# Nine zero products ahead of the first transposes, a last weight chunk of 128 rows, transposes two blocks ahead, and new durations in a hand-written order model

## The chip, the core and the metric

The kernel runs on one core of a Trainium2 chip. The metric is the device time of one execution in microseconds (us). Five engines work side by side, each through its own instructions in order: TensorE (PE, with its weight loads shown as PEld), VectorE (DVE), ScalarE (ACT), GpSimd (POOL) and SyncE (SP), which here issues nearly all DMAs. They meet through semaphores.

## What is computed

The reference normalizes x (2048 rows of 512) and adds two branches to it:

```python
xn = layernorm(x)
# A: attention, 32 heads of 16, each row sees itself and the 255 rows before it
q, k, v = split(xn @ wqkv)
o = softmax(mask(q @ k.T * 16**-0.5)) @ v
# B: gated mixer, 688 columns in each half
z = gelu(xn @ w_in);  z1, z2 = z[:, :688], layernorm(z[:, 688:])
g = w_sp @ z2 + b_sp[:, None]
out = x + o @ wo + (z1 * g) @ w_out
```

Inputs and output are bfloat16.

## The kernel before

The 2048 rows are 16 blocks of 128. The work has three stages.

**Front** (lines 326 to 516). For each block n, VectorE takes the statistics of x (`x_stats`, L387 and L388), adds the epsilon (L259), POOL raises to the power -0.5 (L260), and VectorE applies both (`norm_apply`, L392) and writes `xn`. `transpose_x(n)` turns it to `xnT`: for blocks 0 to 7 by four TensorE transposes (L406) and a ScalarE copy (L409), from block 8 on (`X_DMA = 8`) by a DMA transpose (L401). `do_z(n, half)` multiplies `xnT` by one half of `w_in` (L417; 512 and 176 columns by four chunks) into PSUM tiles of the pool `ps_s`, and ScalarE applies gelu (L425). For the half with z2, VectorE takes statistics (L265) and normalizes (L269). A loop runs n from 2 to 18: the z2 half of block n, the norm of block n + 3, a transpose, the statistics of earlier z2 and later x blocks, one unit of the first k, q, v projections from n = 6 on, and the z1 half of block n - 3. `small_setup` gives POOL three memsets and a small DMA.

**Main stage** (lines 518 to 718). The units are issued in an order that the class `Plan` writes while the program is built:
- `quad(kb, G, e)`: four score products over 32 rows (L623) into two `ps_s` tiles of three, and two exponentials on ScalarE (L631). `mask` clears E on POOL (L640) and, for blocks 0 to 13, on VectorE (L645).
- `unit_av`: 48 small products (L658) into the one bank of `ps_y`, then on VectorE a transpose, a reciprocal, a product and a transpose (L667 to L680).
- `unit_k`, `unit_q`, `unit_v`: projections into the same bank of `ps_y`, read out by VectorE (L290, L310, L324).
- `unit_g(n, hf, c)`: one of 16 products (L545) of half hf of block n of the mixer, 344 columns, into the one bank of `ps_g`; behind the sixteenth VectorE writes `u_sb` (L552) and frees the bank; behind the second half a DMA transpose makes `uT`.
- `unit_out(n, part)`: part 0 adds four products with `wo` (L585), part 1 six with `w_out` (L593) into one `ps_y` bank; VectorE adds x (L597) and SP writes the block. FH is 688, so the last of six chunks has 48 rows.

`Plan` keeps a time for TensorE, VectorE, ScalarE and POOL and adds a constant for each unit. At each step it chooses, among the units whose inputs and bank it takes to be ready, the one of the best rank; `g` products are the filler of the lowest rank. `OUT_MM` is its time of one output product, `self.td += ...` behind an "av" the VectorE time after the bank has been read.

**Tail** (lines 719 to 721). The last three blocks' outputs (`TAIL_OUT = 3`) run behind everything else, in `ps_s` tiles; ScalarE's queue issues their writes.

The buffers of `u_sb` are 768 columns wide and columns 688 to 767 are zero (L379), so that `uT` has zeros in rows 48 to 127 of its last chunk.

Of the kernel before, what the change touches and what calls it, by code (L numbers as in the profile page):

```python
# [8 lines left out]
P = 128  # L9
BF = mybir.dt.bfloat16  # L10
F32 = mybir.dt.float32
# [8 lines left out]
FH = 688  # L20
# [7 lines left out]
NFC = UPAD // P  # L28
# [3 lines left out]
EBUFS = 12  # L32
X_DMA = 8
TAIL_OUT = 3


def nblk(kb):
# [3 lines left out]
class Plan:  # L41
# [1 line left out]

    PROJ = 0.91
    AV_PAIR = 0.0165
    OUT_MM = 0.24
    GCH = 0.144
    LAT = 0.36
    BACK = 0.08
# [13 lines left out]
    def run(self, proj, n_out_inline):  # L63
# [17 lines left out]
        while qi < len(quads) or ai < len(avs) or oi < len(outs) or gi < len(gs) or proj:  # L81
# [13 lines left out]
            if qi < len(quads):  # L95
                kb, G, e = quads[qi]
                ok = True
                if e == 0:
                    i = 4 * kb + G - EBUFS
# [15 lines left out]
            if ai < len(avs):  # L115
                qb, h = avs[ai]
                keys = [(kb, G) for kb in range(max(0, qb - 2), qb + 1) for G in (2 * h, 2 * h + 1)]
                if all(k in masked for k in keys) and not any(
# [3 lines left out]
                    n = sum(1 for k in keys) * 8  # L122
# [8 lines left out]
            if oi < len(outs):  # L131
                n, part = outs[oi]
# [5 lines left out]
            if gi < len(gs):  # L138
                n, hf, c = gs[gi]
# [16 lines left out]
            if pick[2] == "quad":  # L156
                kb, G, e = quads[qi]
                w = nblk(kb)
                order.append(("quad", kb, G, e))
                a, b = (2 * qi) % 3, (2 * qi + 1) % 3  # L160
                dur = {3: 0.755, 2: 0.55, 1: 0.34}[w]
                lat = self.LAT - 0.05 * (3 - w)
                for s in (a, b):
                    self.ta = max(self.ta, self.tp + lat) + dur
                    self.sfree[s] = self.ta + self.BACK
                self.tp += 0.14 + 0.054 * w
                if e == 1:
                    pend.append((self.ta + 0.05, (kb, G)))
                qi += 1
            elif pick[2] == "av":  # L170
                qb, h = avs[ai]
                order.append(("av", qb, h))
                self.tp += pick[3]
                self.yfree = self.evac(0.75)
                self.td += 0.85
                if h == 1:
                    o_at[qb] = self.td + 0.1
                av_emitted.add((qb, h))
                ai += 1
            elif pick[2] == "proj":  # L180
                p = pick[4]
                proj.remove(p)
                order.append(("proj", p[2], p[3]))
                self.tp += pick[3]
                self.yfree = self.evac({"k": 1.2, "q": 0.7, "v": 0.7}[p[2]])
                done_proj[(p[2],) + p[3]] = self.yfree
            elif pick[2] == "out":
                n, part = outs[oi]
                order.append(("out", n, part))
                self.tp += pick[3]  # L190
                if part == 1:
                    self.yfree = self.evac(0.7)
                oi += 1
            else:
                n, hf, c = gs[gi]
                order.append(("g", n, hf, c))
                self.tp += self.GCH
                if c == NB - 1:
                    self.gfree = self.evac(0.52)
                    if hf == 1:  # L200
                        u_at[n] = self.gfree + 3.0
                gi += 1
# [6 lines left out]
def kernel(  # L209
# [12 lines left out]
    nc = tc.nc  # L222
# [6 lines left out]
    xnT = pers.tile([P, NDC, S_TOK], BF, name="xnT")  # L229
    wqkv = pers.tile([P, NDC, 3 * D], BF, name="wqkv")  # L230
    wo_sb = pers.tile([P, NDC, D], BF, name="wo_sb")
    w_out_sb = pers.tile([P, NFC, D], BF, name="w_out_sb")
# [16 lines left out]
    ps_s = ctx.enter_context(tc.tile_pool(name="ps_s", bufs=3, space=bass.MemoryType.PSUM))  # L249
    ps_y = ctx.enter_context(tc.tile_pool(name="ps_y", bufs=1, space=bass.MemoryType.PSUM))  # L250
    ps_g = ctx.enter_context(tc.tile_pool(name="ps_g", bufs=1, space=bass.MemoryType.PSUM))
# [60 lines left out]
    def unit_v(n, on_act=False):  # L312
# [10 lines left out]
        else:  # L323
            nc.vector.tensor_copy(out=dst, in_=src)  # L324

    nc.vector.memset(fmask[:], 1.0)
    nc.vector.memset(esel[:], 1.0)
    make_identity(nc, ident[:])
    with tc.tile_pool(name="win_pool", bufs=1) as winp, tc.tile_pool(
        name="xsp", bufs=8  # L330
# [18 lines left out]
        def load_win(half, c0=0, c1=NDC):  # L349
# [15 lines left out]
            out=fmask[:], in_=fmask[:], pattern=[[-1, P]], compare_op=ALU.is_gt,  # L365
# [7 lines left out]
            out=esel[:], in_=esel[:], pattern=[[32, 4]], compare_op=ALU.is_ge,  # L373
            fill=0.0, base=DH - 1, channel_multiplier=-1,
        )
        def small_setup():
            nc.gpsimd.memset(v_ring[:, :, :, 1, :], 1.0)
            for u_sb in u_sbs:
                nc.gpsimd.memset(u_sb[:, FH:UPAD], 0.0)  # L379
            with nc.allow_non_contiguous_dma(reason="tiny bias gather"):  # L380
                nc.gpsimd.dma_start(out=b_bf[:], in_=B_b_sp.rearrange("(n p) -> p n", p=P))

        xn_tiles = {}

# [5 lines left out]
        def norm_apply(n):  # L390
            xn = xnp.tile([P, D], BF, name="xn")
            nc.vector.tensor_scalar(  # L392
                out=xn[:], in0=xs_tiles[n], scalar1=mvx[:, n, 0:1],
                scalar2=rstdx[:, n : n + 1], op0=ALU.subtract, op1=ALU.mult,
            )
            xn_tiles[n] = xn

        def transpose_x(n):
            xn = xn_tiles.pop(n)
            if n >= X_DMA:  # L400
                nc.sync.dma_start_transpose(out=xnT[:, :, n * P : (n + 1) * P], in_=xn[:])  # L401
                return
            pool, tag = (ps_y, "y") if n in (1, 3) else (ps_g, "g")
            tp = pool.tile([P, NDC, P], BF, name="tp", tag=tag)
            for c in range(NDC):
                nc.tensor.transpose(  # L406
                    out=tp[:, c, :], in_=xn[:, c * P : (c + 1) * P], identity=ident[:]
                )
            nc.scalar.copy(out=xnT[:, :, n * P : (n + 1) * P], in_=tp[:])  # L409

        def do_z(n, half):
            zp2 = ps_s.tile([P, 2, 512], F32, name="zs", tag="S")
            zp = zp2[:].rearrange("p a q -> p (a q)")
            f0 = half * FH
            for c in range(NDC):
                for lo, hi in Z_RANGES:
                    nc.tensor.matmul(  # L417
                        zp[:, lo:hi],
                        lhsT=xnT[:, c, n * P : (n + 1) * P],
                        rhs=w_in_sb[:, c, f0 + lo : f0 + hi],  # L420
                        start=(c == 0),
                        stop=(c == NDC - 1),
                    )
            dst = z1_all if half == 0 else z2_all
            nc.scalar.activation(out=dst[:, n, :], in_=zp[:, 0:FH], func=ACT.Gelu_apprx_tanh)  # L425
# [40 lines left out]
        nc.sync.dma_start(  # L466
            out=w_out_sb[:, 0:5, :], in_=B_w_out[0:640, :].rearrange("(c p) n -> p c n", p=P)
        )
        nc.sync.dma_start(out=w_out_sb[0:48, 5, :], in_=B_w_out[640:688, :])
        norm_apply(2)  # L470
        rs_x(3, 4)
        do_z(0, 1)
        norm_apply(3)
        do_z(1, 1)
        small_setup()
        transpose_x(2)
        x_stats(4)
        transpose_x(3)
        rs_x(4, 5)
        nc.vector.tensor_reduce(  # L480
            out=emask[:, 0:1], in_=esel[:], op=ALU.add, axis=mybir.AxisListType.X
# [9 lines left out]
        for n in range(2, NB + 3):  # L491
            if n < NB:
                do_z(n, 1)
            if n + 3 < NB:
                norm_apply(n + 3)
                if n + 3 >= X_DMA:
                    transpose_x(n + 3)
            if 3 <= n < X_DMA - 1:
                transpose_x(n + 1)
            if n == 4:  # L500
                nc.vector.tensor_copy(out=b_all[:], in_=b_bf[:])
            if 1 <= n - 1 < NB:
                z2_side(n - 1)
            if n + 4 < NB:
                x_stats(n + 4)
                rs_x(n + 4, n + 5)
            if n >= 6 and early:
                f, a = early.pop(0)
                f(*a, on_act=True)
            if n >= 3:  # L510
                do_z(n - 3, 0)
# [60 lines left out]
    def unit_out(n, part, tail=False):  # L572
        if part == 0:
            if not tail:
                load_xres(n)
            if tail:
                t = ps_s.tile([P, 2, 512], F32, name="mt", tag="S")
                fo_tiles[n] = t[:, 0, :]
            else:
                t = ps_y.tile([P, 512], F32, name="fo", tag="y")  # L580
                fo_tiles[n] = t[:]
            fo = fo_tiles[n]
            for c in range(NDC):
                oT = oT_tiles[(n, c // 2)]
                nc.tensor.matmul(  # L585
                    fo, lhsT=oT[:, c % 2, :], rhs=wo_sb[:, c, :], start=(c == 0), stop=False
                )
            return
        fo = fo_tiles.pop(n)
        uT = uT_tiles.pop(n)  # L590
        for c in range(NFC):
            kk = P if c < NFC - 1 else FH - (NFC - 1) * P
            nc.tensor.matmul(  # L593
                fo, lhsT=uT[0:kk, c, :], rhs=w_out_sb[0:kk, c, :], start=False, stop=(c == NFC - 1)
            )
        x_ch = x_tiles.pop(n)
        nc.vector.tensor_tensor(out=x_ch, in0=fo, in1=x_ch, op=ALU.add)  # L597
        (nc.scalar if tail else nc.sync).dma_start(out=out2[n * P : (n + 1) * P, :], in_=x_ch)
        if n + 1 < NB - TAIL_OUT:
            load_xres(n + 1)  # L600
# [151 lines left out]
```

## Time and profile before

| what | value |
|---|---|
| time, median of 3 runs | 295.42 us (295.39 to 295.44) |
| profiled execution: time, span | 295.57 us, 293.9 us |
| PE, DVE, ACT, POOL busy in the span | 269.4, 213.9, 218.2, 92.8 us |
| chain of waits, by engine | PE 64%, DVE 25%, issue 4%, POOL 3% |
| front, main stage, tail | to 61.1, 61.1 to 282.9, to 293.9 us |
| output products L593, score products L623, g products L545 | 96, 576, 512 |

The span runs from the first to the last instruction of the profile. The profile shows matmuls with their latency, so they overlap: how fast TensorE goes is seen from one start to the next. In timeline rows the columns are start, length, engine, line, operation, tiles, shape, count, and in brackets the idle time before it and what ended it. A shape of 48*128 is a product over 48 rows into 128 columns of weights; the rest is the moving operand, so that 48x512 means 48 rows by 512 columns. Some matmul records can be missing, so that rows can show a few too few.

### The profile page before, as it was taken

How to read it: one execution, taken by the hardware profiler on the slowest of the kernel's cores; microseconds unless marked ns; L12 is line 12 of the kernel's file. 1: busy time of each engine (PE TensorE's matmuls, PEld its weight loads, DVE VectorE, ACT ScalarE, POOL GpSimd, SP SyncE). 2: the span in 40 equal slices, each digit the busy share in tenths (PEclk: the TensorE clock that was granted, in tenths of full speed). 3: DMA queues.
4: the chain of work that ended last, by engine and by line, in shares of the span. 5: the costliest groups of instructions: out<-in, count | busy, mean ns of one | idle time of the engine just before them, and what ended most of it. 6: DMA issues, size and time to landing. Idle time of an engine off the chain costs nothing.

```text
span 293.9 us, 7526 instructions
## 1 busy us (share of the span) xinstructions
PE 269.4 (92%) x3136; PEld 135.5 (46%) x3168; DVE 213.9 (73%) x412; ACT 218.2 (74%) x314; POOL 92.8 (32%) x102
## 2 busy tenths in 40 slices
PE   1899999999989989999998999999898999999895
PEld 0555544444435444444544453545444554545451
DVE  5877777936877685865788887866869885956681
ACT  2478756588889889988699958783797678798810
POOL 3622222203342234324143323333233312335520
PEclk9999999999999999999999999999999999999999
DMA  7991111800415242332231423144314133545103
GB/s 230 324 284 44 36 38 36 170 12 0 100 19 118 65 72 51 89 85 51 65 74 39 99 44 94 39 97 56 83 36 100 31 70 83 94 38 134 29 4 80
DMA packets 60178, 23.58 MB, mean 80 GB/s; under 512 B 51264, under 2 KB 59632, under 8 KB 60144
## 3 DMA queue, kind: packets, MB, share of 16 engines
q1 hardware_dynamic: 59664, 22.70, 34.0%
q8 instruction: 25, 0.41, 0.6%
q10 hardware_dynamic: 432, 0.39, 0.4%
q0 software_dynamic: 48, 0.00, 0.1%
q14 instruction: 9, 0.07, 0.1%
HBM read 8.41 MB, written 2.10 MB: 36 GB/s over the span
## 4 chain that ended last, share of the span: by engine, by line
PE 64%; DVE 25%; issue 4%; POOL 3%; DMA 2%; ACT 1%; SPq 0%; DVEq 0%
PE gf L545 23%; PE S L623 9%; PE o_t L658 7%; PE fo L593 7%; PE fo L585 4%; PE m L315 4%; DVE st L265 3%; PE m L300 3%; DVE o_norm L673 3%; DVE st L387 3%; DVE o_c L667 3%; PE m L277 3%; DVE E L645 3%; POOL rstdx L260 2%; PE zs L417 2%
## 5 line engine op out<-in xcount | busy, mean ns | idle before, releaser
L631 ACT ACTIVATE E<-S 128x768 bf16<-128x768 f32 (+2 forms) x256 | 178.9, 773 | 38.4 <-issue 22.6
L640 POOL TENSOR_SCALAR_AFFINE_SELECT E<-E 128x1024 bf16<-128x1024 bf16 x64 | 74.7, 1167 | 147.9 <-ACT E L631 122.3
L545 PE MATMUL gf<-z_all,wspT 128*128 128x344 bf16 x512 | 94.6, 311 | 6.1 <-DVE u_sb L552 6.1
L545 PEld LDWEIGHTS <-wspT 128*128 128x128 bf16 x512 | 44.3, 97 | 38.4 <-issue 15.8
L645 DVE TENSOR_TENSOR E<-E,fmask 128x1024 bf16<-128x1024 bf16 x56 | 47.6, 853 | 0.6
L623 PE MATMUL S<-q_ring,k_ring 32*128 32x384 bf16 (+2 forms) x576 | 45.2, 303 | 1.3 <-ACT E L631 1.2
L417 PE MATMUL zs<-w_in_sb,xnT 128*128 128x512 bf16 (+1 forms) x251 | 42.5, 318 | 2.5 <-DMA xnT<-xn 1.3
L425 ACT ACTIVATE z_all<-zs 128x688 bf16<-128x688 f32 x32 | 23.8, 744 | 17.1 <-PE zs L417 17.1
L667 DVE STREAM_TRANSPOSE o_c<-o_t 128x512 f32<-128x512 f32 x32 | 22.9, 715 | 15.2 <-PE o_t L658 14.9
L417 PEld LDWEIGHTS <-xnT 128*128 128x128 bf16 x256 | 22.7, 101 | 20.9 <-DMA xnT<-xn 3.1
L623 PEld LDWEIGHTS <-k_ring 32*128 32x128 bf16 x576 | 14.6, 91 | 38.3 <-issue 36.0
L658 PE MATMUL o_t<-E,v_ring 128*32 128x128 bf16 x1440 | 26.0, 220 | 1.0 <-DVE k_ring L290 0.8
L658 PEld LDWEIGHTS <-v_ring 128*32 128x32 bf16 x1440 | 20.9, 97 | 8.2 <-issue 7.7
L597 DVE TENSOR_TENSOR x_ch<-fo,x_ch 128x512 bf16<-128x512 f32 x13 | 9.0, 692 | 21.2 <-PE fo L593 18.6
L673 DVE TENSOR_TENSOR o_norm<-o_c,rsum 128x256 bf16<-128x256 f32 x32 | 21.4, 668 | 1.1
L593 PE MATMUL fo<-w_out_sb,uT 128*128 128x512 bf16 x78 | 20.4, 382 | 0.0
L552 DVE SCALAR_TENSOR_TENSOR u_sb<-gf,b_all,z_all 128x344 bf16<-128x344 f32 x32 | 17.9, 560 | 1.7 <-PE gf L545 1.5
L290 DVE TENSOR_TENSOR k_ring<-m,emask 128x1024 bf16<-128x1024 f32 x12 | 14.7, 1221 | 5.8 <-PE m L277 5.8
L315 PE MATMUL m<-wqkv,xnT 128*128 128x512 bf16 x53 | 15.9, 381 | 1.1 <-DVE x_ch L597 0.5
L300 PE MATMUL m<-xnT,wqkv 128*128 128x512 bf16 x58 | 16.2, 380 | 0.7 <-DVE v_ring L324 0.3
L277 PE MATMUL m<-xnT,wqkv 128*128 128x512 bf16 x57 | 16.1, 380 | 0.6 <-DVE o_c L667 0.2
L260 POOL TENSOR_TENSOR rstdx<-rs_v,negh 128x1 f32<-128x1 f32 x16 | 8.8, 550 | 23.6 <-DVE rs_v L259 22.2
(51 smaller groups left out, 175.9 us busy)
## 6 DMA issues: line engine op xcount, KB each, us to landing
xs<-in_A_x_dram SPq DMA_DIRECT2D x7, 256.0 KB, 11.3
x_ch<-in_A_x_dram SPq DMA_DIRECT2D x13, 128.0 KB, 2.2
out_dram<-x_ch SPq DMA_DIRECT2D x13, 128.0 KB, 1.7
wqkv<-in_A_wqkv_dram SPq DMA_DIRECT2D x1, 1536.0 KB, 10.9
w_in_sb<-in_B_w_in_dram SPq DMA_DIRECT2D x4, 344.0 KB, 3.9
w_out_sb<-in_B_w_out_dram SPq DMA_DIRECT2D x1, 640.0 KB, 9.8
wo_sb<-in_A_wo_dram SPq DMA_DIRECT2D x1, 512.0 KB, 11.2
xnT<-in_A_x_dram SPq DMA_DIRECT2D x3, 128.0 KB, 3.3
```

The source lines that it names most:

```text
L300: nc.tensor.matmul(m[:], lhsT=wqkv[:, c, G * P : (G + 1) * P], rhs=xnT[:, c, grp * 512 : (grp + 1) * 512], start=(c == 0), stop=(c == NDC ...
L315: nc.tensor.matmul(m[:], lhsT=xnT[:, c, n * P : (n + 1) * P], rhs=wqkv[:, c, 2 * D : 3 * D], start=(c == 0), stop=(c == NDC - 1),)
L417: nc.tensor.matmul(zp[:, lo:hi], lhsT=xnT[:, c, n * P : (n + 1) * P], rhs=w_in_sb[:, c, f0 + lo : f0 + hi], start=(c == 0), stop=(c == NDC ...
L545: nc.tensor.matmul(gf[:, 0:FQ], lhsT=w[:, c, :], rhs=z2_all[:, c, lo : lo + FQ], start=(c == 0), stop=(c == NB - 1),)
L593: nc.tensor.matmul(fo, lhsT=uT[0:kk, c, :], rhs=w_out_sb[0:kk, c, :], start=False, stop=(c == NFC - 1))
L623: nc.tensor.matmul(S[:, i, d0 : d0 + w], lhsT=k_ring[32 * s : 32 * s + 32, G, e, k0 : k0 + P], rhs=q_ring[32 * s : 32 * s + 32, G, s0 : s0 ...
L631: nc.scalar.activation(out=E[:, 0:nb, j : j + 3 : 2, :].rearrange("p b h c -> p h b c"), in_=tiles[pr][:, :, 0:ncol].rearrange("p h (b c) ...
L640: nc.gpsimd.affine_select(out=E[:, 0, :, :], in_=E[:, 0, :, :], pattern=[[0, 8], [1, P]], compare_op=ALU.is_ge, fill=0.0, base=0, channel_ ...
L645: nc.vector.tensor_tensor(out=E[:, 2, :, :], in0=E[:, 2, :, :], in1=fmask[:].unsqueeze(1).to_broadcast([P, 8, P]), op=ALU.mult,)
L658: nc.tensor.matmul(T[32 * s : 32 * s + 32, e, g2 * P : (g2 + 1) * P], lhsT=v_ring[:, kb % VRING, 4 * G + s, e : e + 2, :].rearrange("p a d ...
L667: nc.vector.transpose(out=C[:, 0 : 32 * DH], in_=T[:].rearrange("p e q -> p (e q)"))
L673: nc.vector.tensor_tensor(out=o_n[:], in0=c_o.rearrange("p e q d -> p q e d"), in1=rsum[:].rearrange("p e q -> p q e").unsqueeze(3).to_bro ...
```

## The change

Four edits:
- VectorE first sets 512 columns of `xnT[:, 3, :]` to zero, and TensorE, ahead of its first transpose, multiplies them nine times into a `ps_s` tile that nobody reads.
- POOL sets the last chunk of `w_out_sb` to zero; the DMA then fills its 48 rows as before, and the sixth output product runs over all 128 rows.
- Blocks 2 and 3 are transposed one z unit earlier each, and in the loop block n + 2 instead of n + 1; block 3 now uses `ps_g`. `small_setup` stands later in the text, at the same place among POOL's instructions.
- Two constants of `Plan` change, and with them the order of the units in the main stage. The order keeps the same 735 TensorE units. In the old one 1 g product stands behind the last AV, in the new one 48.

```diff
+N_WARM = 9
...
-    OUT_MM = 0.24
+    OUT_MM = 0.222
...
-                self.td += 0.85
+                self.td += 1.3
...
+    nc.vector.memset(xnT[:, 3, 0:512], 0.0)
     nc.vector.memset(fmask[:], 1.0)
...
+        nc.gpsimd.memset(w_out_sb[:, NFC - 1, :], 0.0)
...
+        wt = ps_s.tile([P, 2, 512], F32, name="warm_t", tag="S")
+        for i in range(N_WARM):
+            nc.tensor.matmul(
+                wt[:, 0, :], lhsT=xnT[:, 3, 0:P], rhs=xnT[:, 3, 0:512], start=True, stop=True
+            )
...
-            pool, tag = (ps_y, "y") if n in (1, 3) else (ps_g, "g")
+            pool, tag = (ps_y, "y") if n == 1 else (ps_g, "g")
...
         do_z(0, 1)
+        transpose_x(2)
         norm_apply(3)
         do_z(1, 1)
+        transpose_x(3)
         small_setup()
-        transpose_x(2)
         x_stats(4)
-        transpose_x(3)
...
-            if 3 <= n < X_DMA - 1:
-                transpose_x(n + 1)
+            if n + 2 < X_DMA:
+                transpose_x(n + 2)
...
-            kk = P if c < NFC - 1 else FH - (NFC - 1) * P
             nc.tensor.matmul(
-                fo, lhsT=uT[0:kk, c, :], rhs=w_out_sb[0:kk, c, :], start=False, stop=(c == NFC - 1)
+                fo, lhsT=uT[:, c, :], rhs=w_out_sb[:, c, :], start=False, stop=(c == NFC - 1)
             )
```

New line numbers used below: the zero products are L389, transposes L416, z products L427, g products L555, output products L595 and L602, score products L633.

More of the change, by code (lines that the diff above doesn't have):

```diff
@@ L468 @@
         )
-        nc.sync.dma_start(out=w_out_sb[0:48, 5, :], in_=B_w_out[640:688, :])
+        nc.sync.dma_start(out=w_out_sb[0 : FH - 5 * P, 5, :], in_=B_w_out[5 * P : FH, :])
         norm_apply(2)
```

## The prediction

> **What bounds the kernel now.** I read the windows by stage first, then the timeline of TensorE and VectorE in the front stage, TensorE's waits, single products of L593, and the tail. The program has three stages: the front (to 61.1 us: norms, transposes, z products), the main stage written out by Plan (61.1 to 282.9), and the tail (three outputs).
>
> ```profile
> 11.20:25.00 13.80, 12.83 (x97) 7.62 (x98) 10.83 (x36) 9.68 (x16) 4.31 (x8) 1.00 0.88 248
> 39.00:53.50 14.50, 13.39 (x79) 6.90 (x82) 11.58 (x35) 8.46 (x13) 3.49 (x6) 1.00 0.19 37
> 61.10:282.90 221.80, 209.88 (x2783) 104.00 (x2807) 163.34 (x261) 180.94 (x258) 74.67 (x64) 1.00 0.31 65
> ```
>
> The columns are length, busy PE, PEld, DVE, ACT, POOL, granted clock, DMA share and GB/s. In the main stage PE is busy for 209.9 of 221.8 us: an instruction less on PE shortens it, unless PE then waits. In the front stage it is otherwise:
>
> ```profile
> 7.53 4.32 PE L417 MATMUL zs<-w_in_sb,xnT 128*128 128x512 bf16 x16
> 13.16 2.51 PE L417 MATMUL zs<-w_in_sb,xnT 128*128 128x512 bf16 x16 [0.86 <-ACT xnT L409]
> ...
> 39.04 1.34 PE L417 MATMUL zs<-w_in_sb,xnT 128*128 128x512 bf16 x7 [0.38 <-DMA xnT<-xn]
> ...
> 53.48 1.34 PE L417 MATMUL zs<-w_in_sb,xnT 128*128 128x512 bf16 x8 [0.49 <-DMA xnT<-xn]
> ```
>
> ```profile
> 49.76 0.15 DVE L259 TENSOR_SCALAR rs_v<-mvx 128x1 f32<-128x1 f32 x1
> 50.57 0.41 DVE L392 TENSOR_SCALAR xn<-xs,mvx,rstdx 128x512 bf16<-128x512 bf16 x1 [0.66 <-POOL rstdx L260]
> ```
>
> The first 16 z products take 4.32 us, the next 16 take 2.51: the clock is low at first (full clock from 11.2 us by these starts). But from block 11 to block 15 PE waits for xnT each time. Each xnT comes from VectorE's norm (0.41 us, held 0.66 us by the pow on POOL), whose turns come every 3.4 to 3.9 us, and a DMA transpose of 2.4 us. VectorE in this chain waits for POOL only, never for PE. So the front ends by the chain DVE, POOL, DMA: the last norm at 50.57, xnT at 53.48, then 7.6 us of PE work to 61.15.
>
> **1. Nine zero products, and transposes earlier.** A new memset of 128x512 goes first on VectorE. The 128x128 one took 0.17 us, so at most 0.7; VectorE was idle for 1.88 us before 2.96, waiting for xs. fmask and esel come later by that; the activation that reads esel began only at 2.10, after its table load. The nine products are 512 wide; in the slow rows a 512 and a 176 column product together take 4.32/8 = 0.54, so 0.40 to 0.43 each, 3.9 us: from about 1.6 to 5.5, where the first transpose began at 5.25. That is 0 to 0.4 us late, and PE then had 1.27 us idle. In return the first z products may run at the fast rate: 4.32 - 2.51 = 1.8 us, plus up to 0.9 us of the wait for ACT at 13.16, which the new order fills. With blocks transposed two ahead PE asks for xn earlier: blocks 4 to 7 get xn at 12.4, 14.8, 18.1 and 22.0 (VectorE's times, unchanged), so PE waits there and starts step 6 about 1 us later than now. All this lies ahead of the waits at blocks 11 to 15: the five rows' starts lie 0.54, 0.34, 0.46, 0.17 and 0.65 us behind the PE work before them, 2.2 us in all. PE may be up to 2.2 us later, or any amount earlier, at 36 us, and the front still ends at 61.15. **I take 0**; bounds -2.7 (all of it reaches the end) and +0.4.
>
> [...]
>
> **2. The last chunk of w_out on 128 rows.** POOL's memset of 128x512: the 128x1024 one took 0.95 us, so about 0.5, after esel at 2.82, before POOL's next work at 4.14: hidden. The small DMA of this chunk is issued at 16.3, far behind it. Beside VectorE's stats it could cost up to 0.3 us, and VectorE waits 0.61 us for xs at 5.86 anyway. On PE:
>
> ```profile
> 138.53 1.57 PE L593 MATMUL fo<-w_out_sb,uT 128*128 128x512 bf16 x6
> 140.04 0.34 PE L623 MATMUL S<-q_ring,k_ring 32*128 32x384 bf16 x4
> ```
>
> ```profile
> 139.72 0.39 PE L593 MATMUL fo<-w_out_sb,uT 48*128 48x512 bf16 x1
> ```
>
> A 512 column product starts the next 0.216 us later (L585 at 285.39, L593 at 286.26: four in 0.87). Here five take 139.72 - 138.53 = 1.19, that is 4 x 0.216 + 0.32: going from 128 to 48 rows costs 0.10. From 48 to the 32 rows of a quad takes 0.32, from a 128 row product to a quad also 0.31, so that one stays. Before a 128 row product it goes too: in the tail 285.39 - 285.07 = 0.32 against 0.216. In the new order 12 of the 13 inner outputs are followed by a quad and one by g: 12 x 0.10 + 0.20 = **-1.4 us**; the tail is below. Bounds: 0 (if PE only waits longer behind it) and -3.2 (16 x 0.20).
>
> [...]
>
> **3. The new order.** Only OUT_MM and the VectorE time behind AV change in Plan. By the order of the two programs:
> - Groups of adjacent quads fall from 127 to 123. A quad between g products costs 0.10 going in (242 against 146 ns from g to S) and about 0.10 out: 4 x 0.20 = **-0.8 us**.
> - Waits. TensorE's own in the main stage:
>
> ```profile
> PE gf L545 <- DVE u_sb L552: 6.1, 10, 1.3
> PE S L623 <- ACT E L631: 1.2, 4, 0.4
> PE fo L585 <- DVE k_ring L290: 0.9, 1, 0.9
> PE o_t L658 <- DVE k_ring L290: 0.8, 1, 0.8
> ```
>
> (total us, times, longest). They arise where a half of g ends soon behind an AV (whose VectorE chain is 0.72 + 0.25 + 0.67 + 0.45 = 2.1 us) and only one or two PE pieces lie before the next half, or where two users of the one bank of ps_y are close. At 209.91 an AV ends 0.44 us before the half: 2.1 - 0.44 + 0.35 + 0.56 (u_sb) - 1.6 of work between gives 1.0; measured 1.3. (Half n.h is half h of block n.) Counted so, places over 0.5 us cost 11.1 now (start to start, from 78 to 273 us). In the new order: half 3.1 behind AV 3.0, 1.3; k to O at block 0, 0.9; q to AV 5, 0.8; k to AV 7, 0.8; k to v 12, 1.0; halves 8.1 and 12.0, 0.63 each as now; half 12.1, behind AV 13.0 with three quads in a row, 2.0; half 14.0, 0.9; seven smaller, 1.3. The three worst of now (halves 10.0, 10.1 and 3.0) are gone. New is the end: after AV 15.1 come 48 g alone, three halves on one bank; each switch waits 0.31 + 0.05 + 0.53 + 0.05 - 0.15 = 0.8, twice 0.8. Sum 11.8: **+0.7 us**. Bounds: -5 (half of all VectorE waits gone) and +5 (each new place as dear as the dearest now plus ACT's pace: 16 E at 0.70 are 11.2 us in each of blocks 0 to 13, and the PE work between quads falls to 11.6 in block 4 and 10.3 in block 13).
>
> **4. Tail.**
>
> ```profile
> 282.88 0.32 PE L545 MATMUL gf<-z_all,wspT 128*128 128x344 bf16 x1
> 284.50 0.45 DVE L680 STREAM_TRANSPOSE oT<-o_norm 128x256 bf16<-128x256 bf16 x1
> 284.87 0.53 DVE L552 SCALAR_TENSOR_TENSOR u_sb<-gf,b_all,z_all 128x344 bf16<-128x344 f32 x1
> 288.82 1.57 PE L593 MATMUL mt<-w_out_sb,uT 128*128 128x512 bf16 x6
> ```
>
> Now the last AV holds u_sb back; the last six products start 5.94 us behind the last g. With 48 g behind the last AV, u_sb starts 0.36 behind that g and uT is there 4.3 us behind it (0.53, then 3.4 as now). PE needs 0.2 + 2 x 2.16 + 0.86 = 5.4, so PE bounds: -0.56, and -0.10 for the last chunk: **-0.7 us**. Bounds 0 and -0.8.
>
> Sum: 0 - 1.4 - 0.8 + 0.7 - 0.7 = -2.2 from the profiled execution's 295.57 (span 293.9): 293.4. That execution is 0.15 above the median of the runs, so **293.3 us**.
>
> **Rivals.**
> - A, the forecast: padding and fewer quad groups gained, front hidden, waits about equal; 292.0 to 294.8. 42%.
> - B, the new order also removes half of the VectorE waits (about 10 us with the ps_y ones), since AV's 2.1 us is now counted nearly in full: 293.3 - 5 = 288.3 to 292. For it: the worst waits stand behind AV. Against: my count place by place. 23%.
> - C, the start gain reaches the end: 293.3 - 2.7 = 290.6. It needs the norms to come earlier, and no VectorE row waits for PE there. 7%.
> - D, no difference: the padding's gain is eaten by waits behind it, or the edit does not do what it says (the 0.10 stays with 128 rows): 294.8 to 296.0. 12%.
> - E, slower: quads come denser, the filler is spent late, so PE waits for E, and 48 g run alone at the end. Price: each half without filler 0.8, each triple of quads up to 2, block 13 bound by ACT at 11.2 against 10.3 of PE work, 0.9. It decides when added waits pass 0.7 + 2.8: 296 to 298. 16%.
>
> Faster by over 0.2% (0.6 us, about what a measurement can tell from none): 42 + 23 + 7 = 72%; same 12%; slower 16%. The range 290.3 to 296.6 leaves out the far part of B and of E, some 20%.
>
> **What would show it.** Right: xnT(15) still about 53.5 and the first S about 61.1, though the early z products run 1.8 us faster; the six L602 products start every 0.216 and the quad behind them 0.31 later; waits of gf on u_sb 5 to 7.5 us, two of them among the last 48 g; the last six products bound by PE. Wrong: first S earlier than 60; waits on u_sb below 4 or above 9; 0.31 before the last chunk still there.

## The result, and the profile after

The changed kernel takes 297.70 us (median of 20 executions, 296.21 to 298.49) against 295.39 for the kernel before (20, 294.88 to 296.51): ratio 1.0067 [1.0052, 1.0082]. It is slower by 0.67%, so rival E came, and the time lies 1.1 us above the range of the forecast. The profiled execution took 297.95 us, with a span of 296.2 (before 295.57 and 293.9).

The executions fall in two groups, 7 at 296.2 to 296.7 us and 13 at 297.7 to 298.5 (medians 296.35 and 297.95); the profiled one belongs to the second, and in it TensorE's clock is halved once for 3.4 us in the main stage. All 13 have a mean granted clock of 0.994 or 0.988, six of the 7 have 1.000. "At full clock" below means the group with the lower times among a kernel's executions.

The front and the tail moved little, the main stage grew (S is the tile of the score products, so the first S is the first score product):

| stage, us | before | after |
|---|---|---|
| front, to the first S | 61.15 | 61.25 |
| main stage, to the last g | 221.73 | 224.20 |
| tail, to the end | 10.99 | 10.80 |

First TensorE's timeline in the front of the changed kernel (start, length, line, tiles, count, in brackets the idle time and its releaser; the profile has the score products at L632, not L633):

```profile
1.26 4.02 PE L389 MATMUL warm_t<-xnT 128*128 128x512 bf16 x9 [1.26 <-DVE xnT L327]
...
7.63 2.50 PE L427 MATMUL zs<-w_in_sb,xnT 128*128 128x512 bf16 x8
10.32 1.33 PE L427 MATMUL zs<-w_in_sb,xnT 128*128 128x512 bf16 x8
...
53.58 1.34 PE L427 MATMUL zs<-w_in_sb,xnT 128*128 128x512 bf16 x8 [0.51 <-DMA xnT<-xn]
...
61.25 0.34 PE L632 MATMUL S<-q_ring,k_ring 32*128 32x384 bf16 x4
```

Behind the zero products the first eight z products still take 2.50 us, the next eight 1.33: the clock opened at 10.27, before at 11.2. The wait for the last xnT and the first S stand where they stood (53.48 and 61.15 before).

TensorE's waits in the changed kernel (us in total, times, longest):

```profile
PE gf L555 <- DVE u_sb L562: 4.7, 10, 0.8
PE S L632 <- ACT E L640: 3.3, 7, 0.7
...
PE mt L602 <- DMA uT<-u_sb: 0.4, 1, 0.4
```

The waits on u_sb fell from 6.1 to 4.7, those on ScalarE rose from 1.2 to 3.3. This view counts idle time against modelled ends. From one start to the next, all that lies over 0.12 us beyond a product's own rate sums in the main stage (without the 3.4 us of half clock) to about 14.9 us before and 18.4 after: on u_sb 7.0 and 5.9, on ScalarE between quads 3.4 and 6.6, behind readers of the ps_y bank 4.5 and 5.5, on a mask of POOL 0 and 0.6.

The costliest place, in the timeline of TensorE:

```profile
251.72 0.85 PE L667 MATMUL o_t<-E,v_ring 128*32 128x128 bf16 x48
252.50 0.47 PE L555 MATMUL gf<-z_all,wspT 128*128 128x344 bf16 x2
252.90 0.34 PE L632 MATMUL S<-q_ring,k_ring 32*128 32x384 bf16 x4
253.53 0.28 PE L632 MATMUL S<-q_ring,k_ring 32*128 32x256 bf16 x2 [0.29 <-ACT E L640]
254.24 0.28 PE L632 MATMUL S<-q_ring,k_ring 32*128 32x256 bf16 x2 [0.42 <-ACT E L640]
254.94 0.28 PE L632 MATMUL S<-q_ring,k_ring 32*128 32x256 bf16 x2 [0.42 <-ACT E L640]
255.43 0.28 PE L632 MATMUL S<-q_ring,k_ring 32*128 32x256 bf16 x2 [0.21 <-ACT E L640]
255.68 1.28 PE L555 MATMUL gf<-z_all,wspT 128*128 128x344 bf16 x5
256.89 0.40 PE L632 MATMUL S<-q_ring,k_ring 32*128 32x256 bf16 x4
257.23 1.47 PE L667 MATMUL o_t<-E,v_ring 128*32 128x128 bf16 x48
```

Three quads follow one another. Each pair of S products waits until ScalarE has read a ps_s tile, about 0.70 us per pair; where nothing is waited for, the next product starts 0.25 us behind a pair (255.43 to 255.68). Then the same AV that took 0.85 at 251.72 takes 1.47: the clock. By windows (length, busy PE, PEld, DVE, ACT, POOL, granted clock, DMA share, GB/s):

```profile
250.00:256.00 6.00, 4.66 (x81) 2.24 (x80) 4.19 (x9) 5.59 (x10) 2.08 (x2) 1.00 0.12 38
256.00:259.50 3.50, 3.50 (x63) 1.94 (x62) 1.36 (x2) 2.37 (x5) 1.19 (x2) 0.51 1.20 98
259.50:262.00 2.50, 2.50 (x20) 1.10 (x19) 1.12 (x3) 2.06 (x5) 1.09 (x1) 1.00 0.60 132
```

And the end:

```profile
276.94 2.49 PE L555 MATMUL gf<-z_all,wspT 128*128 128x344 bf16 x16 [0.81 <-DVE u_sb L562]
...
280.10 2.49 PE L555 MATMUL gf<-z_all,wspT 128*128 128x344 bf16 x16 [0.67 <-DVE u_sb L562]
...
283.26 2.49 PE L555 MATMUL gf<-z_all,wspT 128*128 128x344 bf16 x16 [0.67 <-DVE u_sb L562]
...
285.80 0.58 DVE L562 SCALAR_TENSOR_TENSOR u_sb<-gf,b_all,z_all 128x344 bf16<-128x344 f32 x1 [2.58 <-PE gf L555]
...
286.46 1.46 PE L602 MATMUL mt<-w_out_sb,uT 128*128 128x512 bf16 x6
...
287.94 1.21 SPq L569 DMA_TRANSPOSE uT<-u_sb  x1
...
291.30 1.47 PE L602 MATMUL mt<-w_out_sb,uT 128*128 128x512 bf16 x6 [0.36 <-DMA uT<-u_sb]
```

The 48 g run as three halves on one bank, each behind a switch. u_sb of block 15 is written by 286.38, yet its DMA transpose starts at 287.94, right behind the six products that began at 286.46. Those read uT(13), and uT has two buffers: block 15 waits for the one of block 13.

### The profile page after: what moved, and what is told of

Its sections match the earlier page's. It is cut to its first block, busy times and chain, and to the rows that moved or that the text cites. A ratio compares the mean times of both kernels' runs of the same rounds, so it can differ in the third digit from the quotient of the medians.

```text
span 296.2 us, 7580 instructions
## 1 busy us (share of the span) xinstructions
PE 273.9 (92%) x3177; PEld 137.4 (46%) x3177; DVE 211.3 (71%) x413; ACT 218.2 (74%) x314; POOL 92.6 (31%) x103
## 4 chain that ended last, share of the span: by engine, by line
PE 64%; DVE 23%; issue 3%; DMA 3%; POOL 3%; ACT 2%; SPq 0%; DVEq 0%; ACTq 0%
PE gf L555 25%; PE S L632 10%; PE o_t L667 7%; PE fo L602 6%; PE fo L595 4%; PE m L316 4%; PE m L301 3%; DVE st L266 3%; DVE E L654 3%; PE m L278 3%; DVE st L397 3%; ACT E L640 2%; POOL rstdx L261 2%; PE zs L427 2%; DVE u_sb L562 2%
## 5 line engine op out<-in xcount | busy, mean ns | idle before, releaser
L649 POOL TENSOR_SCALAR_AFFINE_SELECT E<-E 128x1024 bf16<-128x1024 bf16 x64 | 73.9, 1155 | 142.5 <-ACT E L640 122.2
L555 PE MATMUL gf<-z_all,wspT 128*128 128x344 bf16 x512 | 94.1, 312 | 4.8 <-DVE u_sb L562 4.7
L555 PEld LDWEIGHTS <-wspT 128*128 128x128 bf16 x512 | 44.0, 98 | 37.3 <-issue 15.7
L632 PE MATMUL S<-q_ring,k_ring 32*128 32x384 bf16 (+2 forms) x576 | 45.6, 304 | 3.4 <-ACT E L640 3.3
L654 DVE TENSOR_TENSOR E<-E,fmask 128x1024 bf16<-128x1024 bf16 x56 | 46.7, 834 | 0.8 <-ACT E L640 0.2
L427 PE MATMUL zs<-w_in_sb,xnT 128*128 128x512 bf16 (+1 forms) x256 | 41.9, 315 | 0.8 <-DMA xnT<-xn 0.8
L632 PEld LDWEIGHTS <-k_ring 32*128 32x128 bf16 x576 | 14.7, 91 | 43.7 <-issue 41.2
L427 PEld LDWEIGHTS <-xnT 128*128 128x128 bf16 x256 | 22.7, 100 | 17.5 <-DMA xnT<-xn 1.8
L667 PE MATMUL o_t<-E,v_ring 128*32 128x128 bf16 x1440 | 26.8, 223 | 1.7 <-DVE q_ring L311 0.6
L562 DVE SCALAR_TENSOR_TENSOR u_sb<-gf,b_all,z_all 128x344 bf16<-128x344 f32 x32 | 18.1, 564 | 8.8 <-PE gf L555 8.8
L682 DVE TENSOR_TENSOR o_norm<-o_c,rsum 128x256 bf16<-128x256 f32 x32 | 19.7, 614 | 1.1
L602 PE MATMUL fo<-w_out_sb,uT 128*128 128x512 bf16 x78 | 19.1, 381 | 0.0
L278 PE MATMUL m<-xnT,wqkv 128*128 128x512 bf16 x64 | 16.5, 380 | 1.0 <-DVE k_ring L291 0.7
L316 PE MATMUL m<-wqkv,xnT 128*128 128x512 bf16 x64 | 16.5, 380 | 0.9 <-DVE k_ring L291 0.9
L301 PE MATMUL m<-xnT,wqkv 128*128 128x512 bf16 x64 | 16.5, 380 | 0.3 <-DVE o_c L676 0.3
## 6 DMA issues: line engine op xcount, KB each, us to landing
wo_sb<-in_A_wo_dram SPq DMA_DIRECT2D x1, 512.0 KB, 10.5
```

The costliest lines, as they stand in the source:

```text
L278: nc.tensor.matmul(m[:], lhsT=wqkv[:, c, D + G * P : D + (G + 1) * P], rhs=xnT[:, c, grp * 512 : (grp + 1) * 512], start=(c == 0), stop=(c ...
L301: nc.tensor.matmul(m[:], lhsT=wqkv[:, c, G * P : (G + 1) * P], rhs=xnT[:, c, grp * 512 : (grp + 1) * 512], start=(c == 0), stop=(c == NDC ...
L316: nc.tensor.matmul(m[:], lhsT=xnT[:, c, n * P : (n + 1) * P], rhs=wqkv[:, c, 2 * D : 3 * D], start=(c == 0), stop=(c == NDC - 1),)
L427: nc.tensor.matmul(zp[:, lo:hi], lhsT=xnT[:, c, n * P : (n + 1) * P], rhs=w_in_sb[:, c, f0 + lo : f0 + hi], start=(c == 0), stop=(c == NDC ...
L555: nc.tensor.matmul(gf[:, 0:FQ], lhsT=w[:, c, :], rhs=z2_all[:, c, lo : lo + FQ], start=(c == 0), stop=(c == NB - 1),)
L562: nc.vector.scalar_tensor_tensor(out=u_sb[:, lo : lo + FQ], in0=gf[:, 0:FQ], scalar=b_all[:, n : n + 1], in1=z1_all[:, n, lo : lo + FQ], o ...
```

## The experiments

In this section E is the tile of exponentials that ScalarE writes, and the theories have letters of their own. Theory T: the new order is what makes the kernel slower, by TensorE's waits (ScalarE behind adjacent quads, the one bank at the end); padding and start do what the prediction said. Rivals: the halved clock is the whole loss; or an edit other than the order costs. Kernels of one group share a chip and the runs of the kernel before.

**The old order under the other edits, and the new order alone.**

```diff
-    OUT_MM = 0.222
+    OUT_MM = 0.24
...
-                self.td += 1.3
+                self.td += 0.85
```

> The changed kernel with Plan's two constants of before, so with the old order; zero products, earlier transposes and the 128-row chunk stay. Theory T (the new order alone made it slower): padding gives 13 x 0.10 us and some 0.2 in the tail, the front still ends at 61.2, no stretch of half clock in the main stage: 293.6 to 294.2 us, 0.5% faster than before. Rival R (the padding's gain is swallowed by the next wait, or the start edits cost something): 295.2 us or more.

Measured 293.74 us (11 executions), 0.994 [0.9921, 0.996] of the kernel before. The reverse edit made to the kernel before:

> The kernel before with Plan's two new constants alone; no zero products, no padding, old transposes. Theory T: the changed kernel's 297.7 us plus the 1.4 us that padding gave there: 298.8 to 299.5 us, the three quads in a row before the 13th block of g's halves show ACT waits of 0.5 us each, and many executions have one 3.4 us stretch of half clock behind them. Rival R (the order is harmless, the other edits cost): 295.0 to 295.8 us.

Measured 298.72 (6), 1.0104 [1.008, 1.0129]. The order costs 3.96 us on the one base (297.70 against 293.74, from two groups of runs whose kernel before differs by 0.2) and 3.1 on the other; all that was gained came without it. At full clock, too, the order costs 296.35 - 293.6 = 2.75 (the middles of those groups): the clock is not the whole loss. Waits from start to start: 14.3 us with the old order, 18.1 with the new one alone.

**Padding alone and start alone**, each made to the kernel before (main lines only; POOL's memset, VectorE's memset and the places of blocks 2 and 3 go with them):

```diff
-            kk = P if c < NFC - 1 else FH - (NFC - 1) * P
...
-                fo, lhsT=uT[0:kk, c, :], rhs=w_out_sb[0:kk, c, :], start=False, stop=(c == NFC - 1)
+                fo, lhsT=uT[:, c, :], rhs=w_out_sb[:, c, :], start=False, stop=(c == NFC - 1)
```

> The kernel before with the last chunk on 128 rows alone. Theory T: 13 x 0.10 us in the main stage and about 0.1 in the tail, 295.5 - 1.4 = 294.1 us. Rival (the gain seen with the old order came from the start edits): 295.3 us or more.

Measured 294.21 (7; before 295.60): -1.4 us, 0.9954 [0.9931, 0.9977].

```diff
...
+            wt[:, 0, :], lhsT=xnT[:, 3, 0:P], rhs=xnT[:, 3, 0:512], start=True, stop=True
...
-            if 3 <= n < X_DMA - 1:
-                transpose_x(n + 1)
+            if n + 2 < X_DMA:
+                transpose_x(n + 2)
```

> The kernel before with the zero products and the earlier transposes alone; old order, last chunk on 48 rows. Theory F (the front ends by the norms on VectorE and the DMA transposes): the first score product stays at 61.1 to 61.6 us and the time at 295.3 to 295.7 us. Rival (a warm clock and earlier transposes reach the end): 293.5 us or less.

Measured 295.00 (12), 0.9986 [0.9965, 1.0006]: no difference that the interval shows. The first S starts at 61.09 (61.15 before): the front is hidden.

**The triple of quads.** First, zero products that fill the waits: two more accumulate zeros into the first S tile of four quads, so that S stays what it was.

```diff
+FILL = {(13, 3, 0), (13, 3, 1), (14, 0, 0), (14, 0, 1)}
...
+                    nc.tensor.matmul(
+                        S[:, i, 0:ncol], lhsT=zw[:], rhs=wo_sb[:, 0, 0:ncol], start=False, stop=True
```

> The changed kernel, and in the four quads around that place two products with zero weights are added into the first score tile (the sums stay the same). TensorE does more there, the order stays. Theory C (the clock halves because TensorE streams in only a third of a 3.4 us stretch): the granted clock stays 1.000 in all executions, the times lie in one group at 296.2 to 296.8 us. Rival (the clock drop has another cause, such as a point in time): two groups as before, 296.4 and 298.0, median 297.7 us or more.

Measured 297.60 (6), 1.0067 [1.0048, 1.0087]; five of the six lie within 0.5 us, and the granted clock of the profiled execution is 1.00 from 61.2 to 284.3 us:

```profile
250.00:256.00 6.00, 5.28 (x80) 2.31 (x79) 3.50 (x8) 4.79 (x8) 1.09 (x1) 1.00 0.13 41
256.00:259.50 3.50, 3.50 (x72) 2.08 (x72) 2.45 (x4) 3.45 (x8) 2.18 (x2) 1.00 0.36 73
```

The clock stayed up, as wanted, but the time missed its expectation: the zero products stand in the chain of score product, E, next score product, and the E of quad (14, 0, 0) comes at 255.84 instead of 254.73. The 1.1 us took most of what the clock gave: at full clock the changed kernel takes 296.35. So the run shows no gain, and theory C not either: the profile has no half clock at this place, but two of the six executions have a mean clock of 0.992 and 0.993, and that the share of streaming decides was an estimate of mine (last section). Then the same units in another order, with AV and g between the quads:

```diff
+    i = order.index(("quad", 13, 3, 0))
+    was = order[i : i + 14]
+    put = (0, 3, 4, 5, 1, 2, 6, 9, 10, 11, 7, 8, 12, 13)
+    order[i : i + 14] = [was[p] for p in put]
```

> The changed kernel with 14 units of the order exchanged: the AV of block 13 and three g products are put between the three quads in a row. Theory C with T: ACT's four waits of 0.5 us shrink to about half, TensorE streams more, no half clock: 295.0 to 296.0 us. Rival (the loss is spread over the order, and the clock has another cause): 297.0 us or more.

Measured 297.14 (6), 1.0055 [1.0034, 1.0075]: again short of the expectation. In the profile the AVs at 253.07 and 256.60 take 0.85 us each, so the clock is full there, and the waits on ScalarE in the triple are down to 0.37 and 0.15 us, but the output of block 12 now stands too close behind an AV:

```profile
258.58 0.29 PE L632 MATMUL S<-q_ring,k_ring 32*128 32x256 bf16 x4
259.57 1.02 PE L595 MATMUL fo<-wo_sb,oT 128*128 128x512 bf16 x4 [0.70 <-DVE o_c L676]
```

So neither run shows what the waits between adjacent quads are worth by themselves: both broke into the triple, and both take longer than the changed kernel at full clock, by 1.25 and 0.8 us.

**The end.** Three more places for the last halves, in ps_s tiles that no quad needs any longer:

```diff
-            gf_tiles[n] = ps_g.tile([P, 512], F32, name="gf", tag="g")
+            if (n, hf) in ((14, 1), (15, 0), (15, 1)):
+                gl = ps_s.tile([P, 2, 512], F32, name="gf", tag="S")
+                gf_tiles[n] = gl[:, 0, :]
+            else:
+                gf_tiles[n] = ps_g.tile([P, 512], F32, name="gf", tag="g")
```

> The changed kernel, and the last three halves of g write into three ps_s tiles, free by then, instead of the one ps_g bank. Theory T (the 48 g products at the end wait 0.83, 0.83 and 0.88 us for u_sb because nothing stands between them): those waits vanish, main stage 2.5 us shorter, 297.7 - 2.5 = 295.2 us (293.8 in executions without the half clock). Rival (the tail is set by the DMA transposes of uT, which then wait for each other): less than 1 us gained, 297 us.

Measured 294.80 (12), 0.9969 [0.9949, 0.9989]; at full clock 293.8 against 296.35, -2.5. The 48 products run in one piece:

```profile
274.57 0.41 PE L671 MATMUL o_t<-E,v_ring 128*32 128x128 bf16 x16 [0.41 <-POOL E L653]
274.91 7.17 PE L559 MATMUL gf<-z_all,wspT 128*128 128x344 bf16 x48
```

So three switches of one bank cost 2.5 us, nearly as much as the order as a whole (2.75). Its other new waits are still there (on ScalarE 3.3 us by the view, as in the changed kernel) and must be about paid for by its fewer groups of quads and by waits on u_sb that it no longer has (2.1 us are left of them, against 6.1 in the kernel before). Next, a third place for uT, in a part of xnT that is free by then:

```diff
+                if n == NB - 1:
+                    uT = xnT[:, 1, 0 : NFC * P].rearrange("p (c q) -> p c q", q=P)
```

> The changed kernel, and uT of block 15 lies in a part of xnT that is free by then, instead of in one of two uT buffers. In the changed kernel its DMA transpose started 1.5 us behind the end of u_sb, at the end of the first tail output. Theory W (it waits for that output to have read the buffer): it starts 0.1 us behind u_sb, the last six products start 0.5 us earlier, 297.2 us. Rival (SP or the DMA queue was late for another reason): unchanged, 297.7 us.

Measured 295.96 (12), 1.0022 [1.0004, 1.0041]; -0.5 at full clock (295.85 against 296.35). The median fell by more, since 4 of these 12 executions and 13 of those 20 lie in the group with the longer time. The tail, 10.26 us, is now bound by TensorE:

```profile
284.13 0.57 DVE L562 SCALAR_TENSOR_TENSOR u_sb<-gf,b_all,z_all 128x344 bf16<-128x344 f32 x1 [2.59 <-PE gf L555]
...
288.24 1.03 PE L598 MATMUL mt<-wo_sb,oT 128*128 128x512 bf16 x4
289.10 1.46 PE L605 MATMUL mt<-w_out_sb,xnT 128*128 128x512 bf16 x6
```

**The two constants apart.** The changed kernel with OUT_MM back at 0.24, and with the VectorE time back at 0.85:

```diff
-    OUT_MM = 0.222
+    OUT_MM = 0.24
```

> The changed kernel with OUT_MM back at 0.24; the longer VectorE time behind AV stays. Its order also ends in 48 g products behind the last AV and has two quads of block 14 in a row. Theory T1 (the longer VectorE time behind AV makes Plan spend the g products late and put quads densely): slow like the changed kernel, 296.5 to 298 us. Rival (the new OUT_MM is what harms): 293.6 to 294.5 us.

```diff
-                self.td += 1.3
+                self.td += 0.85
```

> The changed kernel with 0.85 for VectorE's time behind AV; OUT_MM stays at 0.222. 17 g products stand behind the last AV. Theory T1: near the old order, 293.6 to 294.6 us. Rival: 296.5 us or more.

Measured 297.36 (6), 1.0075 [1.0054, 1.0096], and 297.32 (6), 1.0051 [1.0033, 1.007]. The second missed by 3 us: the guess that the VectorE constant is alone to blame falls. At full clock they take about 297.25 (four executions) and 296.3 (two), against 293.6 with both constants back: each constant alone gives an order that loses 2.7 us or more. With 0.222 alone the order is another one again, with its worst wait near the end (where the first one's order loses is open):

```profile
277.85 0.85 PE L667 MATMUL o_t<-E,v_ring 128*32 128x128 bf16 x48
278.63 0.32 PE L555 MATMUL gf<-z_all,wspT 128*128 128x344 bf16 x1
281.21 3.03 PE L555 MATMUL gf<-z_all,wspT 128*128 128x344 bf16 x12 [2.26 <-DVE u_sb L562]
```

Here a half ends one g behind the AV, and u_sb stands behind the AV's chain on VectorE, as at 282.88 to 284.87 in the kernel before; but there the tail follows, here another half.

**The best of it.** Padding, zero products, earlier transposes and uT(15) in xnT with the old order, and the last AV moved behind the last g:

```diff
-    OUT_MM = 0.222
+    OUT_MM = 0.24
...
-                self.td += 1.3
+                self.td += 0.85
...
+    order.remove(("av", 15, 1))
+    order.append(("av", 15, 1))
```

> Zero products, earlier transposes, 128-row chunk, old order, uT of block 15 in a free part of xnT, and the last AV behind the last g, so that u_sb does not wait for AV's VectorE chain. Theory: the last six products become bound by TensorE and start 0.5 us earlier than with the old order alone, 293.6 - 0.5 = 293.1 us. Rival (the end is set by another wait, such as oT of the last AV): 293.6 us.

Measured 292.91 (4, 292.76 to 293.20), 0.9914 [0.9901, 0.9927]: the fastest here, and within 0.2 of the expectation. The last AV now covers the last u_sb, which no longer waits for its chain:

```profile
277.82 2.51 PE L555 MATMUL gf<-z_all,wspT 128*128 128x344 bf16 x16
280.25 0.85 PE L670 MATMUL o_t<-E,v_ring 128*32 128x128 bf16 x48
280.47 0.53 DVE L562 SCALAR_TENSOR_TENSOR u_sb<-gf,b_all,z_all 128x344 bf16<-128x344 f32 x1
281.03 2.41 SPq L572 DMA_TRANSPOSE xnT<-u_sb  x1
...
286.23 1.46 PE L605 MATMUL mt<-w_out_sb,xnT 128*128 128x512 bf16 x6
```

## Why the prediction was wrong

| term, us | predicted | measured | by |
|---|---|---|---|
| 1, start | 0 | +0.1 | first S 61.15 to 61.25 |
| 2, padding | -1.4 | -1.4 | padding alone |
| 3, groups of quads | -0.8 | not apart | count 127 to 123 only |
| 3, waits | +0.7 | +3.5 | 14.9 to 18.4, start to start |
| 4, tail | -0.7 | -0.2 | 10.99 to 10.80 |
| halved clock | none | +1.6 | the two groups' distance |

With the groups taken at -0.8 the terms make +2.8; the spans differ by 2.4, so 0.4 us stay unassigned.

1. **Start: right.** VectorE, POOL and the DMA transpose still end the front, and neither the zero products nor the earlier transposes reach them. In the changed kernel the clock is full from 10.27 us, 0.95 earlier than before (11.22), and the first S came 0.10 later; that nine products would bring the full clock to all the early z products was an estimate of mine, and the changed kernel does not show it (last section). With the start edits alone the first S came at 61.09. The 0.6 us by which that run's median lies lower (not clear of its interval) would then come from the main stage, where a wait of half a microsecond is gone (last section); the old order under the other edits gained 1.84, padding alone 1.39.

2. **Padding: right**, in mechanism and size. In the timeline after, an output and what follows it:

```profile
110.96 1.47 PE L602 MATMUL fo<-w_out_sb,uT 128*128 128x512 bf16 x6
112.36 0.34 PE L632 MATMUL S<-q_ring,k_ring 32*128 32x384 bf16 x4
```

Six products and the step to the quad take 1.40, that is 5 x 0.216 + 0.32; before 140.04 - 138.53 = 1.51.

3. **Waits: this step failed.** The term of +0.7 came to some +3.5. The mechanism was named, in this step's +5 bound and in rival E; its size was off. The places I listed by name came out about as listed: halves 3.1, 8.1, 12.0, 12.1 and 14.0, three places behind a k, one behind a q and two switches at the end sum to 11.1 us against 10.5 forecast, the triple of quads the worst of them (2.46 for 2.0). The three switches at the end that the bank run takes away are among them (half 14.0, whose wait is the 0.81 at 276.94, and the two behind it). What failed is "seven smaller, 1.3": about 14 more places cost some 7.3 us. The kernel before was counted by its places over 0.5 us alone, 11.1; the smaller ones there, which I left out, come to 3.8. The dearest of the unlisted lie between adjacent quads, of which I had put only the triple into the sum. At half 3.1, too, it is ScalarE that ends the wait, and not u_sb as I had counted (last two rows):

```profile
78.17 0.50 PE L632 MATMUL S<-q_ring,k_ring 32*128 32x384 bf16 x6
79.40 0.34 PE L632 MATMUL S<-q_ring,k_ring 32*128 32x384 bf16 x2 [0.74 <-ACT E L640]
...
116.10 0.50 PE L632 MATMUL S<-q_ring,k_ring 32*128 32x384 bf16 x6
117.34 0.34 PE L632 MATMUL S<-q_ring,k_ring 32*128 32x384 bf16 x2 [0.74 <-ACT E L640]
```

Two more are a k right behind a k (0.79 at 161.8) and an AV that waits for a mask on POOL (0.58 at 275.1). I took fewer groups of quads as a gain of 0.8 at no price, but a group grows by a quad that has no filler ahead of it, and ScalarE's 0.70 per E then ends last: the waits on ScalarE grew by 3.2 us by this count, all others together by 0.3. That they would be won back if the quads were apart is not shown; what the runs show by taking waits away is the 2.5 us of the switches.

The condition I gave for E, added waits over 3.5, was just reached; at full clock the loss is 0.96 us, and E's 296 to 298 took in the medians of both groups. At full clock the time would lie just inside my range (296.35 against 296.6); the half clock of step 5 puts the median outside. The fault in the forecast's weights was to let a place-by-place count with an open remainder decide 42 to 16.

4. **Tail: right about the chain, wrong about a buffer.** I let the last DMA transpose follow u_sb at once. It waited 1.5 us for the six products that read uT(13). In the old tail u_sb was written so late, at 285.40, that these readers ended at about the same time and the wait didn't show:

```profile
283.90 1.56 PE L593 MATMUL mt<-w_out_sb,uT 128*128 128x512 bf16 x6
285.49 1.21 SPq L559 DMA_TRANSPOSE uT<-u_sb  x1
```

A third place gave the missing 0.5 back: the tail then takes 10.26, which is the 0.7 that I had forecast.

5. **Clock: not foreseen.** I treated 1.00 as given in the main stage. The stretch of 3.41 us (256.03 to 259.45) costs 1.6 us, and 13 of 20 executions have the longer time. In the 3.41 us ahead of it TensorE's gaps are 0.42 us at most, while gaps of 1.29 us in the kernel before have no half clock behind them; what brings it is not shown (last section).

My own signs: of the early z products half ran faster, eight of the first 16, as the clock opened at 10.27 only; the first S, the 0.216 steps and the quad 0.32 later came as said; the u_sb waits, 4.7 by the view and 5.9 by starts, lie at the edge of 5 to 7.5. "The last six products bound by PE" did not come. None of the signs under "wrong" looked at ScalarE, where the waits grew most, or at the clock.

## What to carry to other kernels

A change to a hand-written order has to be costed over every place where an engine waits, not over the worst ones, and by the same threshold in both kernels; the remainder here was worth more than the change. When groups are merged to save switches between them, ask which engine paces the inside of a group: here a switch was priced at 0.2 us, and a quad without filler waited 0.7 to 1.2 from start to start. At the end of a program, where filler has run out, more banks or a third buffer can be worth nearly as much as a better order (2.5 and 0.5 us here, the order 2.75).

## What the runs showed of the hardware

- In the trace of the changed kernel the granted clock is full from 10.27 us for 245.76, then half for 3.413 and full for another 37.55; in the kernel before it is full from 11.22 for 283.31. Divided by 3.413, the three full stretches give 72.0, 11.0 and 83.0. The profiled executions of the old order, of the new order alone and of each constant alone have a mean clock of 0.994, like the changed kernel's, which fits one such half stretch each. With the old order four g products from 273.13 took 1.33 us and the AV at 274.62 took 1.47, where 0.76 and 0.85 are the times at full clock. With OUT_MM alone the g products behind a wait of 2.26 us are slow (12 in 3.03 us from 281.21; 16 take 2.49 at full clock).
- What brings the half clock stays open. In the 3.413 us ahead of the drop of the changed kernel no wait is over 0.42 us, and TensorE streamed columns for 0.34 of the time; ahead of the slow g products of the old order it was 0.40 to 0.44 of a stretch as long (269.7 to 273.1), with no wait over 0.34. In the kernel before, the 3.413 us from 218.4 have 0.41 and a wait of 1.29, and no half clock follows. The shares are estimates from the traces: 0.216 us for 512 columns, the step of the output products; S products that run side by side (four start within 0.01 us at 252.90 in the changed kernel) counted once; and one projection product that the records of the kernel before lack, added.
- Nine zero products didn't fix when the clock opens. In the changed kernel it is full from 10.27 us, 5 us behind them, and four transposes took 0.61 us at 5.21 and at 7.23. In the split run they took 0.40 at 5.24 and at 7.20, 0.63 at 9.17 and 0.39 at 11.66: full, half and full again. The windows row of that run:

```profile
8.10:11.30 3.20, 3.20 (x16) 1.80 (x14) 2.47 (x7) 1.34 (x3) 2.80 (x5) 0.50 0.96 299
```

- With the start edits alone a wait of about half a microsecond is gone (0.51 us at 248.50 in the kernel before, 0.59 at 247.39 with padding alone): the x add of the twelfth output starts 1.32 us behind its last product in the kernel before and 1.40 with padding alone, but 0.04 with the start edits alone. SP's DMA transpose just ahead took 2.01 and 1.32 us in the former, 1.22 with the start edits alone. Why is not settled.
- The product by rsum on VectorE (L682, L673 in the kernel before) took 1.35 and 1.26 us instead of 0.43 at 271.22 and 274.69, where POOL writes a mask (L649, 1.09 us from 271.21 and from 274.58); that lengthens an AV's chain by 0.8 to 0.9. It is so in both kernels: of 64 such products, the 19 that took 0.48 to 1.35 us all began while a mask was running, and each ended 0.27 to 0.28 us behind that mask's end; the five that began 0.21 to 0.22 us ahead of a mask took 0.42. The two dearest waits of the kernel before (from 209.91 and 220.16) stand behind such products of 1.33 us, at 209.22 and 219.47. The 0.67 in my chain of 2.1 us behind an AV is a mean over both kinds.
